# Grouped-query decode attention on one core: the V loads issued from GpSimd's queue, the K loads left on SyncE's

## The chip, the cores and the metric

The kernel runs on one core of a Trainium2 chip. The metric is the device time of one execution in microseconds (us); the text uses us throughout and MB for 10^6 bytes, MiB for 2^20. A profiled execution is read beside it: its span, engine by engine, and the DMA traffic. Engines are called TensorE (PE), VectorE (DVE), ScalarE (ACT), GpSimd (POOL) and SyncE (SP); 16 DMA engines move the data between the device's memory and the on-chip memory.

## The reference

Two sequences, one new token each. The token is normalised and goes through attention over a cache of 32768 keys and values, and through a small gated MLP; the results are multiplied and added to the token.

```python
# x (2,1,512); k_cache, v_cache (2, 8, 32768, 128) float32; 32 query heads, 8 K/V heads
xn = layernorm(x)
q  = (xn @ wq) split into 32 heads of 128
scores = q . k_cache * 128**-0.5          # 4 query heads share one K/V head
o  = softmax(scores) . v_cache
s  = o (all heads side by side) @ wo      # (4096, 512)
gate = xn @ W_gate ; gate = gate * (gate > 0)
g  = silu((gate * (xn @ W_up)) @ W_down)  # width 1792
out = x + s * g
```

Everything is float32. K and V together are 537 MB, read once; the weights are another 27 MB.

## The kernel before, in words

**Groups, tiles and pairs.** There are 16 groups, one for each sequence and K/V head. A group's 32768 tokens are 4 tiles of 8192. Tiles are handled two at a time: a *pair* j holds tiles 2j and 2j+1, so a group is two pairs and there are PAIRS = 32 of them. One load brings the K (or the V) of a whole pair, 8 MiB: 128 partitions with 64 KB each, in one contiguous piece per partition (`rows_of`, line 413).

**Buffers.** K has two buffers of 8 MiB, `kbuf[0]` and `kbuf[1]`, used in turn by even and odd pairs. V has one, `wide`. Before the first V, `wide` also serves the query weights `wq`, then the MLP's `W_gate` and `W_up`, then `W_down`. At the end the V of pair 30 goes into `kbuf[0]`, which has no more K to hold, and the output weights `wo` go into `kbuf[1]`, cut into six loads.

**A step.** The loop of line 882 takes one pair of scores and one pair of sums over V per step; sums run two pairs behind scores. In step j:

- VectorE transposes the K of pair j in place, 8 pieces (`k_transpose`, line 657), TensorE multiplies them with the query (`scores`, line 662);
- TensorE adds up the V of pair j-2 with the softmax weights (`values`, line 739);
- VectorE takes the scores out (`take_scores`); in every odd step a group is complete, and its maximum, its exponentials (ScalarE) and the sums and output of the group before follow (`tile_maximum`, `sums`, `maximum`, `take_o`, `finish_group`);
- the weights of the next sums are multiplied out on TensorE and transposed on VectorE (`weights`, `take_weights`).

**What GpSimd does.** In odd steps it forms the query of the next group (`take_query`, line 526, after the last scores of the old one) and copies a finished group's output into `ots` (line 810). Besides some preparation at the start it has nothing else.

**What sets the order.** Each operation is recorded by `Program.op` with the keys that it reads and writes; from these the class derives the semaphore waits. Each engine executes its own operations in the order in which they were recorded, and an operation that has to wait holds up all that come behind it on the same engine. A load is an operation of the engine that issues it: that engine waits until the destination is free, then hands the load to its DMA queue. The loads are recorded through one helper, with SyncE as the engine unless another is given:

```python
def load(dst, src, sem, r=(), w=(), engine="SP"):
    pg.op(engine, lambda e: e.dma_start(dst, src), r, w, dma=sem)
```

In step j the loads are recorded at the end of the step: the V of pair j-1 (`load_vv(j - 1)`, into `wide`, free once `values` of pair j-2 is done), then the K of pair j+2 (`load_kk(j + 2)`, free once `scores` of pair j is done). In step 30 the V of pairs 29 and 30 are loaded, in step 31 the V of pair 31 and `wo`. Only the two small loads of x at the start are issued elsewhere, by ScalarE.

## Time and profile before

| | |
|---|---|
| runs, median of 3 (lowest to highest) | 1309.91 us (1309.86 to 1310.29) |
| span of the profiled execution | 1308.4 us |
| bytes read | 564.67 MB, 432 GB/s over the span |
| busy, share of the span | TensorE 859.0 us (66%), VectorE 718.1 us (55%), ScalarE 51.4 us (4%), GpSimd 10.5 us (1%) |
| K loads | 32, median 48.2 us from issue to landing |
| V loads into `wide` | 31, median 29.6 us from issue to landing |

The profiled execution has no time of its own besides its span; the median of the runs is 1.5 us above that span.

How to read the lines that follow. A line of the timeline has the start and the busy time in us, the engine, the line of the kernel, the operation, its output and input, and in brackets the idle time before it with what ended it. Line 240 is `load`, line 243 is `mm`, so every load and nearly every matmul carries one of these numbers, and one tells them apart by their tiles: `s<-k,qcur` are scores, `o<-w,wt` and `o<-k,wt` are sums over V, `m_ps` is a scratch bank. `SPq` and `ACTq` are the issues of loads on SyncE's and ScalarE's queues; their duration is that of the issue, not of the transfer. The lines by slice cut the span into 40 equal parts and give the busy share in tenths. A line of the windows gives a stretch, its length, the busy time of PE, its weight load, VectorE, ScalarE and GpSimd with their counts, then the granted clock, the DMA share and GB/s.

### The profile page before, as it was taken

What the parts mean: (1) busy time and instruction counts of PE and PEld (TensorE: products, weight loads), DVE (VectorE), ACT (ScalarE), POOL (GpSimd) and SP (SyncE); (2) the same over time, 40 slices, a digit from 0 to 9 for tenths busy, and PEclk for the clock granted to TensorE, in tenths of its full rate; (3) what the DMA queues carried; (4) which work ended last, traced back from release to release, by engine and by line L of the source; (5) the groups of instructions that cost most, each with busy time, mean ns of one, the idle gap of its engine ahead of it and who ended that gap; (6) DMA issues with size and microseconds to landing.
All of it is one profiled execution on the core that took longest, in us unless ns stands there. A gap on an engine that the chain in (4) does not pass through costs nothing.

```text
span 1308.4 us, 11146 instructions
## 1 busy us (share of the span) xinstructions
PE 859.0 (66%) x4720; PEld 211.5 (16%) x4720; DVE 718.1 (55%) x690; ACT 51.4 (4%) x133; POOL 10.5 (1%) x38
## 2 busy tenths in 40 slices
PE   3566675785666587576667667667665757865676
PEld 1111111211111121111111112121111112111121
DVE  3566654565655456664546666455665545656521
ACT  0001000000000000000000000000000000000000
POOL 0000000000000000000000000000000000000000
PEclk9677788878878887878898778798887889788788
DMA  9999999999999999999999999999999999999998
GB/s 417 423 438 435 437 431 441 425 439 429 437 429 439 435 433 441 429 441 427 439 429 437 429 439 435 433 441 429 441 427 439 429 437 429 439 435 433 439 431 357
DMA packets 10693, 564.79 MB, mean 432 GB/s; under 512 B 1195, under 2 KB 1211, under 8 KB 1597
## 3 DMA queue, kind: packets, MB, share of 16 engines
q1 hardware_dynamic: 10668, 564.67, 99.7%
q8 instruction: 6, 0.10, 0.0%
q14 instruction: 3, 0.02, 0.0%
q10 hardware_dynamic: 16, 0.01, 0.0%
HBM read 564.67 MB, written 0.00 MB: 432 GB/s over the span
## 4 chain that ended last, share of the span: by engine, by line
DMA 64%; DVE 17%; PE 15%; issue 4%; SPq 0%
DMA k<-in_A_k_cache_dram 58%; DVE k L660 17%; PE o L243 8%; PE s L243 6%; DMA k<-in_A_wo_dram 3%; DMA w<-in_A_wq_dram 2%; PE m_ps L243 1%; PE m_ps L693 0%; PE d L243 0%; SPq L240 0%; DVE gy L870 0%; DVE gy L872 0%
## 5 line engine op out<-in xcount | busy, mean ns | idle before, releaser
L243 PE MATMUL s<-k,qcur 128*32 128x512 f32 x2048 | 504.5, 710 | 370.5 <-DVE k L660 370.3
L660 DVE STREAM_TRANSPOSE k<-k 128x2048 f32<-128x2048 f32 x256 | 565.2, 2275 | 147.0 <-DMA k<-in_A_k_cache_dram 147.0
L243 PE MATMUL o<-w,wt 128*16 128x512 f32 x1984 | 245.5, 596 | 9.0 <-DMA w<-in_A_v_cache_dram 9.0
L243 PEld LDWEIGHTS s<-k,qcur 128*32 128x32 f32 x2048 | 89.5, 123 | 785.0 <-DVE k L660 639.3
L737 DVE STREAM_TRANSPOSE wt<-pt 128x512 f32<-128x512 f32 x64 | 45.9, 717 | 139.4 <-PE pt L243 134.6
L678 DVE TENSOR_SCALAR_CACHE_REDUCE st<-s 128x512 f32<-128x512 f32 x64 | 43.0, 672 | 120.9 <-PE s L243 120.9
L243 PEld LDWEIGHTS o<-w,wt 128*16 128x16 f32 x1984 | 62.4, 98 | 167.5 <-issue 167.5
L722 ACT ACTIVATE st<-st,nb 128x512 f32<-128x512 f32 x64 | 45.4, 710 | 1111.0 <-DVE nb L719 1111.0
L243 PE MATMUL pt<-st,perm 128*128 128x512 f32 x128 | 72.6, 696 | 1.5 <-ACT st L722 1.5
L763 DVE RECIPROCAL rl<-m_ps 128x1 f32<-128x1 f32 x16 | 2.7, 169 | 111.0 <-PE m_ps L243 111.0
L243 PE MATMUL m_ps<-ob,heads 128*128 128x128 f32 x128 | 21.7, 321 | 29.0 <-DVE ob L777 29.0
L243 PEld LDWEIGHTS pt<-st,perm 128*128 128x128 f32 x128 | 25.3, 219 | 34.4 <-issue 30.1
L803 DVE STREAM_TRANSPOSE os<-m_ps 128x512 f32<-128x512 f32 x16 | 11.5, 717 | 23.2 <-PE m_ps L243 23.2
L243 PEld LDWEIGHTS m_ps<-ob,heads 128*128 128x128 f32 x128 | 18.0, 217 | 31.1 <-DVE ob L777 31.1
L243 PE MATMUL m_ps<-w,wt 128*32 128x512 f32 (+1 forms) x128 | 16.2, 640 | 8.1 <-DMA w<-in_A_wq_dram 8.1
L777 DVE SCALAR_TENSOR_TENSOR ob<-o,share,ob 128x128 f32<-128x128 f32 x48 | 16.9, 351 | 1.7
L530 POOL TENSOR_TENSOR qcur<-qall,block_of 128x128 f32<-128x128 f32 x16 | 6.5, 406 | 1008.3 <-PE s L243 974.0
L243 PE MATMUL m_ps<-negone,mrow 1*128 1x1 f32 x32 | 6.0, 256 | 9.3 <-DVE mrow L708 9.3
L722 ACT ACTIVATION_READ_ACCUMULATOR st<-st,nb 128x1 f32 x64 | 11.9, 186 | 0.0
L481 DVE COPY os<-m_ps 128x512 f32<-128x512 f32 x2 | 1.4, 692 | 16.3 <-PE m_ps L243 16.3
L243 PE MATMUL o<-k,wt 128*16 128x512 f32 x64 | 8.4, 687 | 2.8 <-DMA k<-in_A_v_cache_dram 2.8
L391 PE MATMUL m_ps<-ident,st 32*128 32x32 f32 x4 | 0.7, 307 | 14.0 <-DVE st L380 14.0
(80 smaller groups left out, 102.8 us busy)
## 6 DMA issues: line engine op xcount, KB each, us to landing
k<-in_A_wo_dram SPq DMA_DIRECT2D x1, 4096.0 KB, 37.3
w<-in_B_W_gate_dram SPq DMA_DIRECT2D x1, 3584.0 KB, 19.6
w<-in_B_W_up_dram SPq DMA_DIRECT2D x1, 3584.0 KB, 27.6
w<-in_B_W_down_dram SPq DMA_DIRECT2D x1, 3584.0 KB, 15.6
k<-in_A_wo_dram SPq DMA_DIRECT2D x1, 2048.0 KB, 41.7
k<-in_A_wo_dram SPq DMA_DIRECT2D x1, 1024.0 KB, 43.7
k<-in_A_k_cache_dram SPq DMA_DIRECT2D x32, 48.2
k<-in_A_wo_dram SPq DMA_DIRECT2D x1, 512.0 KB, 44.5
```

The source lines that it names most:

```text
L243: return lambda e: e.matmul(out_, lhs, rhs, start=start, stop=stop, skip_group_check=True)
L391: lambda e, k=k: e.transpose(px[:, k * 32 : (k + 1) * 32], xquad[:, k, :], ident[:32, :32])
L481: dve(lambda e, q=qs, h=half: e.tensor_copy(q, pq[h]), [f"m{half}"], [f"os{half}"])
L530: lambda e: e.tensor_tensor(qcur.rearrange("p e (k h) -> p e k h", h=REP), qall[:, b, hk].unsqueeze(2).to_broadcast([P, 4, Q // REP, REP]) ...
L660: dve(lambda e: e.transpose(at_, at_), [f"k{t // 2 % 2}"], [key])
L678: lambda e: e.tensor_scalar(st[u], ps_s[t % 2], SCALE, None, op0=ALU.mult, op1=ALU.max, accum_out=mx[:, u : u + 1],),
L722: lambda e, u=u: e.activation(st[u], st[u], AF.Exp, bias=nb, scale=1.0, accum_out=ls[:, u : u + 1]),
L737: dve(lambda e: e.transpose(wt[t % 2], ps_p[t % 2]), [f"pt{t % 2}"], [f"wt{t % 2}"])
L763: dve(lambda e: e.reciprocal(rl, ps_m[1][:, :1]), ["m1"], ["rl"])
L777: lambda e, part=part, c=c: e.scalar_tensor_tensor(ob, part, share[:, c : c + 1], ob, op0=ALU.mult, op1=ALU.add),
L803: lambda e: e.transpose(ot, ps_m[1].rearrange("p (h q j) -> p j h q", h=REP, j=ROWS)),
```

## The change

The loads into `wide` that bring V are issued by GpSimd instead of SyncE. The loads of a step are gathered in `load_next` and recorded right behind the sums over V, ahead of the work that takes the scores out, instead of at the end of the step. Thereby a V load stands on GpSimd's queue behind the sums over V that it waits for and ahead of the copy into `ots`. The K loads, the V load of pair 30 (into `kbuf[0]`), the MLP's weights and `wo` stay on SyncE's queue, where no V load stands between them any more. Nothing else is changed: the same bytes go into the same buffers with the same waits.

```diff
         if 2 * j == NK - 4:
             load(kbuf[0], rows_of(vc, 2 * j), "k0", w=k_keys(0))
         else:
-            load(wide, rows_of(vc, 2 * j), "v", w=["wide"])
+            load(wide, rows_of(vc, 2 * j), "v", w=["wide"], engine="POOL")
...
+    def load_next(j):
+        if j == 0:
+            load_d()
+        elif j < PAIRS - 1:
+            load_vv(j - 1)
+        if j == PAIRS - 2:
+            load_vv(PAIRS - 2)
+        if j + 2 < PAIRS:
+            load_kk(j + 2)
+        if j == PAIRS - 1:
+            load_vv(PAIRS - 1)
+            load_wo()
+
...
         if summed:
             values(v)
             values(v + 1)
+        load_next(j)
         if live:
             take_scores(s)
             take_scores(s + 1)
...
             for t in (v + 2, v + 3):
                 weights(t)
                 take_weights(t)
-        if j == 0:
-            load_d()
-        elif j < PAIRS - 1:
-            load_vv(j - 1)
-        if j == PAIRS - 2:
-            load_vv(PAIRS - 2)
-        if j + 2 < PAIRS:
-            load_kk(j + 2)
-        if j == PAIRS - 1:
-            load_vv(PAIRS - 1)
-            load_wo()
```

## The prediction

> **What bounds the kernel now.** I read the page first, its slices and its chain, then the issues on SyncE's queue in order of time, then one pair of steps engine by engine, then the start.

> ```profile
> span 1308.4 us, 11146 instructions
> DMA  9999999999999999999999999999999999999998
> q1 hardware_dynamic: 10668, 564.67, 99.7%
> HBM read 564.67 MB, written 0.00 MB: 432 GB/s over the span
> DMA 64%; DVE 17%; PE 15%; issue 4%; SPq 0%
> w<-in_A_v_cache_dram SPq DMA_DIRECT2D x31, 29.6
> k<-in_A_k_cache_dram SPq DMA_DIRECT2D x32, 48.2
> w<-in_A_wq_dram SPq DMA_DIRECT2D x1, 21.9
> ```

> All 16 DMA engines are busy in every slice but the last, and one queue, SyncE's, carries practically every byte. Nothing computed sets the pace: the bytes do. So a change in who issues a load can hardly gain; it can lose, if it lets the engines run dry. The next rows are the issues of steps 24 to 26, of the first three V loads and of the last.

> ```profile
> 96.45 0.33 SPq L240 DMA_DIRECT2D w<-in_A_v_cache_dram  x1
> ...
> 137.72 0.33 SPq L240 DMA_DIRECT2D w<-in_A_v_cache_dram  x1
> ...
> 175.83 0.33 SPq L240 DMA_DIRECT2D w<-in_A_v_cache_dram  x1
> ...
> 985.77 0.33 SPq L240 DMA_DIRECT2D w<-in_A_v_cache_dram  x1
> 986.14 0.43 SPq L240 DMA_DIRECT2D k<-in_A_k_cache_dram  x1
> 1025.91 0.33 SPq L240 DMA_DIRECT2D w<-in_A_v_cache_dram  x1
> ...
> 1063.05 0.33 SPq L240 DMA_DIRECT2D w<-in_A_v_cache_dram  x1
> ...
> 1257.88 0.33 SPq L240 DMA_DIRECT2D w<-in_A_v_cache_dram  x1
> 1258.25 2.81 SPq L240 DMA_DIRECT2D k<-in_A_wo_dram  x6
> ```

> Two steps take 1063.05 - 985.77 = 77.28 us and bring four loads of 8 MiB, so a load alone costs the engines 19.32 us, 434 GB/s. Each engine gets 8 partitions of a load, 64 KB each; I call one a row, 19.32 / 8 = 2.415 us. The query weights, the first load and also 8 MiB, took 21.9 us to land: 2.6 us of start and landing lie beside the 19.3.

> In each step V goes out first and K right behind, on one queue, in order. V lands 29.6 us after its issue: it waits about 8 us for the rest of the K load before it, then runs alone. K lands at 48.2, 19 us behind V. Before V is the next K at about 9 us; that order, K, V, K, V, is what the change gives up. What each load has to meet:

> ```profile
> 996.14 17.66 DVE L660 STREAM_TRANSPOSE k<-k 128x2048 f32<-128x2048 f32 x8 [7.74 <-DMA k<-in_A_k_cache_dram]
> 1018.42 0.59 PE L243 MATMUL s<-k,qcur 128*32 128x512 f32 x1
> 1018.42 7.46 PE L243 MATMUL o<-w,wt 128*16 128x512 f32 x61
> 1031.15 1.58 DVE L737 STREAM_TRANSPOSE wt<-pt 128x512 f32<-128x512 f32 x2
> 1034.81 17.67 DVE L660 STREAM_TRANSPOSE k<-k 128x2048 f32<-128x2048 f32 x8 [2.08 <-DMA k<-in_A_k_cache_dram]
> 1055.14 0.61 PE L243 MATMUL o<-w,wt 128*16 128x512 f32 x3
> 1055.56 0.59 PE L243 MATMUL s<-k,qcur 128*32 128x512 f32 x1
> 1064.11 1.58 DVE L737 STREAM_TRANSPOSE wt<-pt 128x512 f32<-128x512 f32 x2 [7.22 <-PE pt L243]
> ```

> Step 25 (odd): transposes begin at 996.14, scores end at 1019.0 (22.9 us), the sums over V end at the next issue, 1025.9 (6.9), VectorE is through the softmax of the group at 1032.7 (6.8). Step 26 (even): 1034.81, scores end at 1056.15 (21.3), sums end at 1063.05 (6.9), VectorE is through at 1065.7 (2.6). Together 67.4 us; the other 9.8 of 77.2 are the two waits for K, 7.74 and 2.08. K therefore has slack. V has almost none: issued at 1025.91 it lands at about 1055.5, and its first matmul stands at 1055.14; the one issued at 985.77 lands at about 1015.4, some 3 us ahead of its use.

> **The change part by part.** *Waits of the loads.* K's buffer is free when the scores end, V's when the sums end. Before, both went out at the end of the sums, for K stood behind V on SyncE. Now K goes out 6.9 us earlier, V where it did. PE, VectorE and ScalarE keep their programs.

> The start shows an issue on a third engine and two queues at work:

> ```profile
> 0.74 0.39 SPq L240 DMA_DIRECT2D w<-in_A_wq_dram  x1
> 1.42 1.19 ACTq L240 DMA_DIRECT2D st<-in_A_x_dram  x1
> 10.13 0.68 DVE L364 TENSOR_REDUCE stat<-st 32x1 f32<-32x512 f32 x1 [2.91 <-DMA st<-in_A_x_dram]
> 22.77 9.20 PE L243 MATMUL m_ps<-w,wt 128*32 128x512 f32 x64 [8.10 <-DMA w<-in_A_wq_dram]
> ```

> *GpSimd's queue.* A V load waits there for the sums. Ahead of it in an odd step is the next query's product, which needs the scores only; behind it stands the copy into `ots`, which needs VectorE's work after the same sums. Nobody waits longer for either: 0. The issue itself has no row on GpSimd. The nearest are 0.33 us on SyncE and 1.19 on ScalarE; I take at most 0.9 us more than now and count it with the 2.6 above. Below 0 it can't be: GpSimd starts no earlier than the sums end. [...]

> *Two queues instead of one.* This is the large term. What a DMA engine does with work on two queues shows only in the rows above. The 4 KB of x, issued behind the weights on ScalarE's queue, are in use at 10.13, while the weights go on until 22.7. The engine does not finish a load before it turns to the other queue; it changes after a row or two. [...] With V and K both waiting I therefore give each every second row, and V half the rate as long as K has rows.

> The steady pair, t = 0 at the end of the sums of an even step. V goes out. K went out 6.9 us ago and has 5 of 8 rows left. Five of each take 24.1 us. The next scores end at 2.6 + 22.9 = 25.5, the next K goes out, and V's last rows (1.4 us alone, then some 2.5 rows alternating with K) end at about 36.5; with 2.6 it lands at 39.1. Sums until 46.0, VectorE until 52.8, scores at 74.1, sums at 81.0 if the V issued at 46.0 is there: K has 1.6 rows left by then, so 9.6 rows and 2.6 us, landed at 71.8. It is. Two steps: **81.0 instead of 77.28, +3.7**. If each turn goes K first and landing costs a row more, 83; if V's turns come first, 79.8. In this pair the engines are dry some 4 us: K has nothing to fetch, both its buffers being full.

> Steps 2 and 3 cost more, as K's rows never run out behind the MLP's weights. V0 goes out at 96.5; 15 rows and 2.6 are 38.8: landed at 135.3 to 138, sums end at 142 to 145 (before: 137.72). V1: the same again, sums end at 188 to 194 (before: 175.83): +12 to +18, I take 16.

> Steps 4 to 31 are 14 pairs: 14 x 3.7 = 52.

> The end: now the last sums of step 31 end at 1257.9, and 50.5 us remain to 1308.4.

> ```profile
> 1286.06 9.01 PE L243 MATMUL o<-w,wt 128*16 128x512 f32 x64 [8.97 <-DMA w<-in_A_v_cache_dram]
> ...
> 1304.21 0.64 PE L243 MATMUL s<-k,ots 128*32 128x128 f32 x16 [0.17 <-DMA k<-in_A_wo_dram]
> ...
> 1306.60 0.69 SPq L240 DMA_DIRECT2D out_dram<-gy  x1
> ```

> Then the output weights go out 6.9 us earlier and V31 is the last to land, 25.8 us after the sums; 9.0 of sums, and 12 to 13.4 from there (before: 1295.1 to 1308.4, the last weights at 1304.2): 47 to 48, so -3.

> Sum: 1308.4 + 16 + 52 - 3 = 1373.4 us of span. The runs' median is 1309.91, 1.5 above the span, so 1374.9. With 79.8 to 83 for a pair and 12 to 18 at the start it is 1354 to 1405. Each landing that comes later than reckoned lengthens the loop and none shortens the rest, so I go 3 us above: **1378**.

> **The rivals.** *V first.* If a packet from GpSimd's queue holds its engine's whole share (8 rows) against single rows of K, V passes everything. V then lands 22 us after issue; K pays: some 10 of the K before it (issued one bare step of 34 us ago, 19.3 of them V's and 5 its predecessor's), two V loads, itself 19.3 and 1.5 to land, 69 us from the end of scores to the transposes two steps later, and 21.3 more: 90.7. The next two steps make do with the bare chain, 67.4. Four steps are 158 instead of 154.6; seven such cycles and a late K at the start, +25 to +55: 1335 to 1365; with packets of 2 to 4 rows both have nearly what they need, 1313 to 1335. For it: V's slack is the smaller. Against: the weights and x changed after a row or two. [...]

> *V starved.* If V's packets are a fraction of a row, K takes nearly all until it is empty. V issued at 0 starts at 12.4, stops at 25.5 for the next K, and lands at 25.5 + 19.3 + 6.2 + 2.6 = 53.6 instead of 39.1: up to 95 us for two steps, +18 in 14 pairs, 1570; with half rows a good third of it, from 1420. Against: both loads have 64 KB in one piece.

> *No change: whole loads in turn.* If an engine takes a load as a whole, V comes behind the rest of K(j+1) and ahead of the K issued 6.9 us before it, exactly as now. It lands 29 to 31 us after issue, and 1307 to 1312 stands. It decides from where V lands within about 31 us. Against: x at 10.13. [...]

> ```profile
> 100.00:138.00 38.00, 28.17 (x150) 6.50 (x145) 22.19 (x21) 4.58 (x10) 0.41 (x1) 0.82 1.01 438
> DVE k L660 <- DMA k<-in_A_k_cache_dram: 147.0, 31, 7.7
> ```

> *Faster.* If two queues close the seams between loads, the rate (last column, GB/s) would have to rise from 434: all bytes at the 438 of this stretch are 12 us less. But the queue is never empty now, and VectorE's 147 us of waits for K are no loss while the engines are full. That the change doesn't do what it says I see no way to: K and V have separate semaphores and buffers.

> **How the numbers follow.** Equal rows 0.53 (1354 to 1405, and to 1425 with landings later than reckoned), V first 0.20, V starved 0.10, no change 0.13, of which 0.01 falls beyond 0.2% on the slow side, faster 0.04. 0.2%, 2.6 us, is about what a measurement of this kernel can tell from no change. Leaving out faster, the low third of no change and nearly all of V starved is 0.17: the range is 1308 to 1430, and equal rows' own is 1354 to 1425. Faster 0.04, same 0.12, slower 0.53 + 0.20 + 0.10 + 0.01 = 0.84.

> **What would show it.** V's time to landing: 37 to 40 us in one step and 24 to 27 in the next (equal rows), 22 throughout (V first, then K at 40 to 70), about 30 (no change). PE's first matmul over V should wait for the V load, some 13 us in every second step, and VectorE's waits for K should be nearly gone (equal rows); DMA's slices should show 8 among the 9s. I am wrong if the engines stay full and V lands within 31 us.

## The result, and the profile after

The changed kernel is slower: the ratio is 1.0994, 95% interval 1.0976 to 1.1012. The profiled execution took 1443.3 us with a span of 1441.7. The median of its four runs, 1454.67, is no measure of the change, as two of them ran at a lower granted clock (0.77 and 0.80 against 0.82), and the ratio leaves those out. By the ratio the change costs some 130 us, 1440 us in place of 1309.9; later sections compare with this 1440. Forecast were 1378 us with a range up to 1430: the right side and the expected mechanism, but only half of its size, 68 us instead of 130.

The page of the changed kernel, then its longest waits on a load (total us, how many, the longest):

```profile
span 1441.7 us, 11146 instructions
DMA  9999998989899897998989899798989989899893
q1 hardware_dynamic: 6204, 304.62, 49.5%
q0 software_dynamic: 4464, 260.05, 42.1%
w<-in_A_v_cache_dram POOLq DMA_DIRECT2D x31, 35.5
k<-in_A_k_cache_dram SPq DMA_DIRECT2D x32, 33.9
...
PE o L243 <- DMA w<-in_A_v_cache_dram: 278.3, 17, 18.4
DVE k L660 <- DMA k<-in_A_k_cache_dram: 14.3, 2, 8.4
```

The bytes are the same, but the engines now have 7s and 8s among their slices. V is on a queue of its own (q0): 31 loads of 128 rows and 16 completions each are 4464 packets, so a V row is still one piece of 64 KB, like K's. The waits have changed sides: VectorE waited 147.0 us for K before, now 14.3; TensorE waits 278.3 us for V, before 9.0 and that at the end. V comes late in every second step, by 17.6 to 18.4 us in all but the first two and the last two of these steps. One pair of steps, GpSimd and TensorE and VectorE in order of time:

```profile
745.30 0.53 POOL L240 DMA_DIRECT2D w<-in_A_v_cache_dram  x1 [29.85 <-PE o L243]
765.24 3.62 PE L243 MATMUL s<-k,qcur 128*32 128x512 f32 x26 [1.15 <-DVE k L660]
768.95 0.40 POOL L530 TENSOR_TENSOR qcur<-qall,block_of 128x128 f32<-128x128 f32 x1 [23.12 <-PE s L243]
786.65 8.73 PE L243 MATMUL o<-w,wt 128*16 128x512 f32 x64 [17.79 <-DMA w<-in_A_v_cache_dram]
795.73 0.59 POOL L240 DMA_DIRECT2D w<-in_A_v_cache_dram  x1 [26.38 <-PE m_ps L243]
802.24 17.62 DVE L660 STREAM_TRANSPOSE k<-k 128x2048 f32<-128x2048 f32 x8
822.95 7.45 PE L243 MATMUL o<-w,wt 128*16 128x512 f32 x61
830.70 0.53 POOL L240 DMA_DIRECT2D w<-in_A_v_cache_dram  x1 [29.83 <-PE o L243]
```

This is the loop of the prediction. V goes out at 745.30 and TensorE begins with it at 786.65, 41.3 us later; the scores were done at 768.9, so it waits 17.8 us. Sums until 795.73, VectorE until 802.24, scores until 823.5, sums until 830.70. Two steps take 85.4 us instead of 77.28. The windows of that pair, and of a stretch just before it, in which K's buffers are both full (share of DMA and GB/s stand last):

```profile
745.30:830.70 85.40, 51.09 (x278) 11.82 (x277) 43.71 (x40) 2.93 (x8) 1.73 (x4) 0.82 0.92 393
...
720.00:738.00 18.00, 14.07 (x74) 2.64 (x76) 15.02 (x9) 0.00 (x0) 0.00 (x0) 0.85 0.69 295
```

The engines work 92% of the pair: the bytes no longer set the pace, the loop through V's one buffer does.

The trace also records the single packets of the DMA engines, and there the turns can be read one by one. From 749.3 on each engine moves a row of V, a row of K, a row of V and so on, 64 KB and 2.42 us each. V's eighth and last row is through by 783.9, a row of K follows, and only then, by 786.3, comes the 4-byte packet that ends V's load; TensorE begins at 786.65. On the way K's queue spends one of its turns, at 771.0 to 771.8, on the 4-byte packet of its own load. Counted from the row that was under way when V was issued, eight rows of K pass beside V's eight.

### The profile page after: what moved, and what is told of

Same layout as the page of the kernel before. It is cut to its first block, busy times and chain, and to the rows that moved or that the text cites. A ratio compares the mean times of both kernels' runs of the same rounds, so it can differ in the third digit from the quotient of the medians.

```text
span 1441.7 us, 11146 instructions
## 1 busy us (share of the span) xinstructions
PE 856.0 (59%) x4720; PEld 205.7 (14%) x4720; DVE 715.5 (50%) x690; ACT 51.4 (4%) x133; POOL 27.9 (2%) x69
## 3 DMA queue, kind: packets, MB, share of 16 engines
q0 software_dynamic: 4464, 260.05, 42.1%
HBM read 564.67 MB, written 0.00 MB: 392 GB/s over the span
## 4 chain that ended last, share of the span: by engine, by line
DMA 52%; issue 28%; PE 15%; DVE 6%; POOL 0%; SPq 0%; POOLq 0%; DVEq 0%
DMA w<-in_A_v_cache_dram 47%; PE o L243 11%; DMA k<-in_A_k_cache_dram 3%; DVE k L660 2%; PE m_ps L243 2%; DMA w<-in_A_wq_dram 2%; DVE ob L777 1%; PE s L243 1%; DVE os L803 1%; DVE ob L771 0%; DVE mrow L708 0%; DVE share L766 0%; PE pt L243 0%; PE m_ps L693 0%; DVE mr L698 0%
## 5 line engine op out<-in xcount | busy, mean ns | idle before, releaser
L243 PE MATMUL s<-k,qcur 128*32 128x512 f32 x2048 | 477.7, 646 | 239.7 <-DVE k L660 239.7
L660 DVE STREAM_TRANSPOSE k<-k 128x2048 f32<-128x2048 f32 x256 | 563.9, 2270 | 14.3 <-DMA k<-in_A_k_cache_dram 14.3
L243 PE MATMUL o<-w,wt 128*16 128x512 f32 x1984 | 260.4, 659 | 278.3 <-DMA w<-in_A_v_cache_dram 278.3
L243 PEld LDWEIGHTS s<-k,qcur 128*32 128x32 f32 x2048 | 84.6, 114 | 631.1 <-DVE k L660 511.4
L243 PEld LDWEIGHTS o<-w,wt 128*16 128x16 f32 x1984 | 60.8, 104 | 466.3 <-DMA w<-in_A_v_cache_dram 285.9
L737 DVE STREAM_TRANSPOSE wt<-pt 128x512 f32<-128x512 f32 x64 | 45.9, 717 | 147.5 <-PE pt L243 141.9
L243 PE MATMUL pt<-st,perm 128*128 128x512 f32 x128 | 68.7, 663 | 1.5 <-ACT st L722 1.5
L243 PE MATMUL m_ps<-ob,heads 128*128 128x128 f32 x128 | 20.4, 307 | 29.2 <-DVE ob L777 29.2
L240 POOL DMA_DIRECT2D w<-in_A_v_cache_dram x31 | 17.5, 565 | 884.4 <-PE o L243 472.9
L243 PEld LDWEIGHTS pt<-st,perm 128*128 128x128 f32 x128 | 23.6, 205 | 32.6 <-issue 27.2
L243 PEld LDWEIGHTS m_ps<-ob,heads 128*128 128x128 f32 x128 | 17.1, 208 | 31.4 <-DVE ob L777 31.4
L243 PE MATMUL m_ps<-w,wt 128*32 128x512 f32 (+1 forms) x128 | 15.4, 612 | 7.9 <-DMA w<-in_A_wq_dram 7.9
L243 PE MATMUL m_ps<-negone,mrow 1*128 1x1 f32 x32 | 6.0, 256 | 10.2 <-DVE mrow L708 10.2
```

Source lines behind the costliest of these rows:

```text
L243: return lambda e: e.matmul(out_, lhs, rhs, start=start, stop=stop, skip_group_check=True)
L660: dve(lambda e: e.transpose(at_, at_), [f"k{t // 2 % 2}"], [key])
L737: dve(lambda e: e.transpose(wt[t % 2], ps_p[t % 2]), [f"pt{t % 2}"], [f"wt{t % 2}"])
```

## The experiments

The theory: with V and K on two queues each engine takes a row of the one, then a row of the other; V, which had no slack, gets half the rate as long as K has rows. Rival 1: GpSimd's way of issuing a load is what is slow. Rival 2: K goes out 6.9 us earlier, ahead of V, and that costs, whatever the queue.

**act_queue.** V by ScalarE instead of GpSimd (ScalarE's loop written out, so that it can hold the loads).

```diff
-            load(wide, rows_of(vc, 2 * j), "v", w=["wide"], engine="POOL")
+            load(wide, rows_of(vc, 2 * j), "v", w=["wide"], engine="ACT")
...
-            pg.emit("ACT", e, sems, loop=(NU, NK))
+            pg.emit("ACT", e, sems)
```

> The V loads are issued by ScalarE instead of GpSimd, at the same place in the order; everything else as in the changed kernel. Theory (two queues take turns row by row, so V runs at half rate while K has rows, and the loop V, sums, softmax, scores, sums grows from 77.3 to 85.3 us per two steps): it makes no difference which second engine issues; 1425 to 1450 us, V landing about 41 us after its issue in every even step. Rival 1 (GpSimd's way of issuing a load is what is slow): back to about 1310. Rival 2 (K issued ahead of V is what costs, whatever the queue): as slow as the changed kernel too.

Measured: 1438.65 us, ratio 1.0963 (1.0941 to 1.0985). V goes out at 747.70 and TensorE begins with it at 789.30: 41.6 us, as from GpSimd. Who issued on the second queue, GpSimd or ScalarE, made no difference here.

```profile
747.70 50.78 ACTq L240 DMA_DIRECT2D w<-in_A_v_cache_dram  x2
...
789.30 8.78 PE L243 MATMUL o<-w,wt 128*16 128x512 f32 x64 [17.75 <-DMA w<-in_A_v_cache_dram]
```

**all_gpsimd.** The other half of that question: one queue, but GpSimd's.

```diff
-        load(kbuf[b], rows_of(kc, 2 * j), f"k{b}", w=k_keys(b))
+        load(kbuf[b], rows_of(kc, 2 * j), f"k{b}" if j < 2 else f"kp{b}", w=k_keys(b), engine="SP" if j < 2 else "POOL")
...
-            load(kbuf[0], rows_of(vc, 2 * j), "k0", w=k_keys(0))
+            load(kbuf[0], rows_of(vc, 2 * j), "kp0", w=k_keys(0), engine="POOL")
```

W_down and wo got `engine="POOL"` in the same way.

> All loads from W_down on (K, V and the output weights) issued by GpSimd, V first and K right behind it as in the kernel before: one queue again, but GpSimd's. Theory (taking turns between two queues is what costs): no second queue, 1308 to 1316 us. Rival 1 (GpSimd's way of issuing costs): well above 1330. Rival 2 (early K): K is not early here, about 1310.

Measured: 1311.87 us, ratio 1.0013 (1.0003 to 1.0022). On the page of this kernel the engines are as full as before, and V and K land after 28.8 and 47.6 us, the same order as on SyncE (29.6 and 48.2):

```profile
DMA  9999999999999999999999999999999999999998
q0 software_dynamic: 9808, 532.16, 93.8%
w<-in_A_v_cache_dram POOLq DMA_DIRECT2D x31, 28.8
k<-in_A_k_cache_dram POOLq DMA_DIRECT2D x30, 47.6
```

Rival 1 falls: GpSimd issues 94% of the bytes and loses 0.1%.

**moved_only.** Only the recording of the loads is moved; V stays on SyncE.

```diff
-            load(wide, rows_of(vc, 2 * j), "v", w=["wide"], engine="POOL")
+            load(wide, rows_of(vc, 2 * j), "v", w=["wide"])
```

> Only the second half of the change: the loads are recorded behind the sums over V, but V stays on SyncE. Every theory: the loads keep their order on SyncE and their waits, so 1308 to 1312 us, as before.

Measured: 1310.04 us, ratio 1.0001 (0.9991 to 1.0010). That half of the change does nothing by itself.

**k_held.** Two queues, but K leaves at the same moment as V, as before the change.

```diff
-        load(kbuf[b], rows_of(kc, 2 * j), f"k{b}", w=k_keys(b))
+        load(kbuf[b], rows_of(kc, 2 * j), f"k{b}", w=k_keys(b), after=["o"])
```

`after` makes the load wait for what last wrote the key, here the sums, and holds up nobody itself; V of pair 30 and wo got it too.

> V on GpSimd's queue as in the changed kernel, but each K load, the V load of pair 30 and the output weights also wait for the sums over V of their step, so that K and V go out at the same moment, as in the kernel before. Theory: V (8 rows) and the K just issued (8 rows) alternate from the first row in every step, V needs 38.6 + 2.6 = 41 us each time, then 9 us of sums: about 50 us a step instead of 42.7, 1570 to 1650 us. Rival 2 (it is the early K that costs): back to about 1310. Rival 1 (GpSimd's issue): about 1440, unchanged.

Measured: 1693.91 us, ratio 1.2915 (1.2893 to 1.2938); forecast were 1570 to 1650.

```profile
718.35 0.59 POOL L240 DMA_DIRECT2D w<-in_A_v_cache_dram  x1 [27.10 <-PE m_ps L243]
...
759.19 9.91 PE L243 MATMUL o<-w,wt 128*16 128x512 f32 x64 [10.43 <-DMA w<-in_A_v_cache_dram]
...
769.44 0.53 POOL L240 DMA_DIRECT2D w<-in_A_v_cache_dram  x1 [45.04 <-PE o L243]
```

V needs 759.19 - 718.35 = 40.8 us, now in every step (8 + 8 rows are 38.6, and 2.6), and a step takes 51.1. Rival 2 falls as the main cause: the early K is the better of the two ways to run two queues. The forecast was short in two ways. Its own 50 us a step in place of 42.7 come to some 1660 us over 30 steps, more than its range allowed; and the step took 1.1 us more than 50, most of it in the sums, 9.9 us here and not 9.

**one_queue_k_first.** K as early as in the changed kernel, on one queue.

```diff
-            load(wide, rows_of(vc, 2 * j), "v", w=["wide"], engine="POOL")
+            load(wide, rows_of(vc, 2 * j), "v", w=["wide"])
...
-        elif j < PAIRS - 1:
-            load_vv(j - 1)
         if j == PAIRS - 2:
             load_vv(PAIRS - 2)
         if j + 2 < PAIRS:
             load_kk(j + 2)
+        if 0 < j < PAIRS - 1:
+            load_vv(j - 1)
```

> All loads on SyncE's queue, but in each step K stands ahead of V: K goes out when the scores end, V behind it when the sums end. So K is as early as in the changed kernel, with one queue. Theory: without a second queue nothing is shared; V stands behind the whole K in the same order of bytes, the queue stays full for the most part and only the end is longer, as V of the last pair now comes behind the output weights: 1320 to 1345. Rival 2 (K ahead of V costs): 1430 or more. Rival 1 (GpSimd's issue): about 1310 to 1330.

Measured: 1353.33 us, ratio 1.0307 (1.0266 to 1.0347), some 8 us beyond what was expected. TensorE waits for V here too:

```profile
PE o L243 <- DMA w<-in_A_v_cache_dram: 174.2, 26, 15.1
```

So rival 2 holds in part: K ahead of V costs 3.1% without any second queue, though not the 1430 us that it would need to explain the change; V then stands behind the whole K of its step. These 3.1% are no share of the 9.9%: on two queues V does not stand behind K but takes turns with it, and there holding K back made the time longer still.

**k_rows_32k, k_rows_16k, v_rows_32k.** The share itself. A load is cut into loads of half or a quarter of the columns, so that its rows have 32 or 16 KB; the bytes stay, and whoever uses a load waits for all its parts. The diff is that of K in halves; quarters, and V in halves, are made alike.

```diff
-        load(kbuf[b], rows_of(kc, 2 * j), f"k{b}", w=k_keys(b))
+        cut = 2 * HALF // 2
+        for i in range(2):
+            at_ = slice(i * cut, (i + 1) * cut)
+            w = k_keys(b) if i == 0 else [f"k{b}+{i}"]
+            load(kbuf[b][:, at_], rows_of(kc, 2 * j)[:, at_], f"k{b}", w=w)
```

> The changed kernel with each K load cut into two loads of half the columns, so that a K row is 32 KB while a V row stays 64 KB; same bytes, same buffers, the transposes wait for both halves. Theory: taking turns row by row now gives V two thirds of the rate instead of half; V needs 8 of its own rows and 8 half rows of K, 29 us, and lands after about 31.6 us instead of 41.3: 1325 to 1345 us. Rival 1 (GpSimd's issue) and rival 2 (early K): about 1440, unchanged, or slightly more for the additional loads.

> The changed kernel with each K load cut into four loads of a quarter of the columns: K rows of 16 KB against V rows of 64 KB. Theory (turns row by row): V gets four fifths of the rate, 10 row times for its 8 rows, and lands after some 27 us; V is then no longer late in most steps, K is slower but has slack: 1325 to 1350 us, less than the 1361 of the halves. If only the number of loads mattered, it would be above 1361.

> The changed kernel with each V load cut into two loads of half the columns (rows of 32 KB) and K whole (64 KB); the sums wait for both. Theory (turns row by row): V gets a third of the rate while K has rows; V issued in an even step lands after about 49 us instead of 41, and the one of the odd step is late too: 85 us a pair become 93 or more, 1530 to 1620 us. If the engines shared by bytes, or if smaller pieces were simply better (as the K halves and quarters might suggest), it would be 1440 or less.

Measured: K's rows at 32 KB 1361.36 us, ratio 1.0392 (1.0362 to 1.0422); at 16 KB 1331.0, 1.0158 (1.0141 to 1.0175); V's at 32 KB 1540.11, 1.1732 (1.1683 to 1.1780). One pair of issue and use from K at 32 KB, and then one from V at 32 KB (an issue there is two loads):

```profile
749.68 0.59 POOL L240 DMA_DIRECT2D w<-in_A_v_cache_dram  x1 [17.77 <-PE m_ps L243]
783.30 9.54 PE L243 MATMUL o<-w,wt 128*16 128x512 f32 x64 [5.83 <-DMA w<-in_A_v_cache_dram]
```

```profile
703.84 1.05 POOL L240 DMA_DIRECT2D w<-in_A_v_cache_dram  x2 [30.48 <-PE o L243]
...
752.55 8.34 PE L243 MATMUL o<-w,wt 128*16 128x512 f32 x64 [25.12 <-DMA w<-in_A_v_cache_dram]
```

From issue to use V takes 33.6 us against half rows of K (31.6 to landing was forecast; the median landing of that run is 32.7), 41.3 against whole ones, and 48.7 when its own rows are halved (49 forecast). Smaller pieces are not better by themselves: halving K's gains 80 us, halving V's loses 100. In these runs the engines took turns by rows, not by bytes, and the load with the smaller rows gave way. The times of the quarters and of V's halves lie in their ranges; the halves of K, 1361 us, were expected at 1345 at most. V was still waited for in 25 of 31 steps there, 168.7 us in all. With K at 16 KB the waits have gone over to K again, in part:

```profile
w<-in_A_v_cache_dram POOLq DMA_DIRECT2D x31, 28.4
DVE k L664 <- DMA k<-in_A_k_cache_dram: 105.3, 14, 15.3
PE o L243 <- DMA w<-in_A_v_cache_dram: 69.5, 17, 16.4
```

It is the best of the kernels with two queues, and still 21 us behind the kernel before, with V and then K on one queue.

**kv_halves.** Both cut at 32 KB, and each half of V (one tile) goes out and is waited for by itself. K's loads are cut as above.

```diff
-        return half_of(wide, t), "wide"
+        return half_of(wide, t), f"wide_v{t % 2}"
...
-            load(wide, rows_of(vc, 2 * j), "v", w=["wide"], engine="POOL")
+            for i in range(2):
+                at_ = slice(i * HALF, (i + 1) * HALF)
+                w = ["wide_v0", "wide"] if i == 0 and j == 0 else [f"wide_v{i}"]
+                load(wide[:, at_], rows_of(vc, 2 * j)[:, at_], f"v{i}", w=w, engine="POOL")
```

> The changed kernel with K and V both cut into two loads of half the columns, one tile each: rows of 32 KB on both queues, K's transposes wait for both halves, but each half of V goes out when the sums of its own tile are done and is waited for by those sums alone. Theory: turns are equal as in the changed kernel, but V's loop gets shorter by the sums of one tile at both ends, 3.5 to 4.5 us each, about 8 us a pair: 85.3 back to 77.3, where the bytes set the pace again: 1315 to 1345 us. If it were the taking of turns as such (lost rate on the engines) and not V's loop, it would stay near 1440.

Measured: 1380.32 us, ratio 1.0535 (1.0517 to 1.0552), some half of the gain that was expected.

```profile
716.75 0.53 POOL L240 DMA_DIRECT2D w<-in_A_v_cache_dram  x1 [26.39 <-PE o L243]
720.18 0.53 POOL L240 DMA_DIRECT2D w<-in_A_v_cache_dram  x1 [2.90 <-PE o L243]
...
759.94 6.14 PE L243 MATMUL o<-w,wt 128*16 128x512 f32 x32 [12.73 <-DMA w<-in_A_v_cache_dram]
766.42 0.53 POOL L240 DMA_DIRECT2D w<-in_A_v_cache_dram  x1 [18.33 <-PE m_ps L243]
```

The first half leaves 3.4 us ahead of the second, as thought, and the rest of the sums takes 6.5 us instead of 9.1. So the loop is V's, and shortening it pays although the turns are equal. But half the matmuls take 70% of the time: 6.14 us for 32, where 64 take 8.7. TensorE is slow after the wait. That accounts for part of the missing gain; the rest stays open.

**pe_kept_busy, pe_busy_18.** Is it the idling? Matmuls of constants fill the wait, 144 and then 18 in each odd step.

```diff
+        if live and ends and j > 2:
+            spin = mm(ps_d[:32, :], fold, heads.rearrange("p h k m -> p (h k m)"), True, True)
+            pe(chain([spin] * 18), ["fold", "heads"], ["d"])
         if summed:
             values(v)
```

> The changed kernel with 144 matmuls of constants added on TensorE between the scores and the sums over V of each odd step, into a bank that nobody reads any more: they lie in the some 18 us in which TensorE waits for V. Theory for the sums' 8.8 us instead of 7.1: TensorE starts slowly after the idle time. Then the sums behind the added work take about 7.1, and 1.7 to 2 us go from each pair of steps: 25 to 32 us off the time. Rival (the sums are slow for another reason, such as reading V while K is written): 8.8 us remain and the time too.

> As pe_kept_busy, with the number of added matmuls set by what one of them took there (122.9 us for 144, 0.85 each): 18 of them, 15.4 us, inside the wait of some 18 us. Theory (TensorE starts slowly after idling): the sums over V of odd steps take about 7.4 instead of 8.8 us, 1.4 us for each of 15 pairs: 15 to 25 us off the changed kernel's time. Rival (slow for another reason): no change.

Measured: 3029.6 us with 144, for one takes 0.85 us, and not 0.25 like one of the sums (a pair's sums are 32 matmuls, which the trace lists as 64); 1439.85 with 18, ratio 1.0988 (1.0970 to 1.1006), which is the changed kernel's. One step of the first (the sums follow the added work without a gap), then one of the second:

```profile
875.45 0.61 PE L243 MATMUL o<-w,wt 128*16 128x512 f32 x3
...
875.89 7.44 PE L243 MATMUL o<-w,wt 128*16 128x512 f32 x61
```

```profile
772.82 15.18 PE L243 MATMUL d<-heads,fold 128*32 128x512 f32 x35
...
791.35 8.50 PE L243 MATMUL o<-w,wt 128*16 128x512 f32 x64 [3.35 <-DMA w<-in_A_v_cache_dram]
```

With no gap the 64 take 7.9 us from the first start to the last end (875.45 to 883.33; their first three run among the work before), with one of 3.35 us they take 8.5, with 17.8 us 8.7. The traces of all runs decide between idling and the rival. In all but kv_halves, whose sums come in halves, sums that start by themselves after an idle time of up to 2.0 us take 7.06 us, 23 times of 23 (one_queue_k_first at 710.01, after 1.70 us); after more than 3.5 us they take 8.3 to 10.0, 148 times of 148 (the changed kernel at 1214.10, 8.35 after 18.40 us; k_held at 759.19, 9.91 after 10.43); in between both occur. Sums that follow the scores are short while other loads are being written: the row of 7.45 us at 822.95 of the changed kernel, 61 of the 64, runs beside a DMA share of 0.99. So the idling does it in these runs, and 3 us of it were mostly enough: in 11 of the 13 steps in which the 18 matmuls left some 3 us, the sums still took 8.5 to 8.8, and the expected 15 to 25 us did not come. A filling that ends just as V lands was not tried.

**v0_first.** In step 1 the first V is put ahead of the next query on GpSimd.

```diff
-        elif j < PAIRS - 1:
+        elif 1 < j < PAIRS - 1:
             load_vv(j - 1)
...
                 if t == 2:
                     mlp_down()
+                    load_vv(0)
```

> The changed kernel, but in step 1 the first V load is recorded ahead of the next query's product, so that on GpSimd it waits for the MLP's last product only and not for the scores of the step. Theory: V0 goes out at about 96 us instead of 101.2, lands 5 us earlier, and the loop behind it starts 5 us earlier: 4 to 8 us off the time, as far as that shows. Rival (GpSimd's order costs nothing, as the prediction had it): no difference.

Measured: 1439.61 us, ratio 1.0989 (1.0971 to 1.1008): no difference. In the profiled execution V0 left at 95.60 instead of 101.17 and V1 at 146.81 instead of 153.96, but V2 left at 200.12, no earlier than the 198.47 of the changed kernel. The expectation was wrong: the lead was gone by the third V load. Why is not shown.

## Why the prediction was wrong in size

*What bounds the kernel, and that it could only lose*: right. *Rows in turn*: right, read from the packets themselves and shown from both sides: V is in use after 33.6, 41.3 and 48.7 us as K's rows are half of V's, equal and twice V's. The rivals *V first*, on a packet of 8 rows, *no change*, on whole loads, and *V starved*, on parts of a row, fall with the same three numbers. A full queue brought the same rate from GpSimd, 431 GB/s over the span of all_gpsimd, as from SyncE, 432 before; the time with V and K on two queues rose by 9.9% all the same.

*The steady pair* is the step that failed: 81.0 us forecast, 85.4 measured. Its mechanism was right, and two of its terms were too small, V's landing and, above all, the sums that had to wait for V. By its own terms:

| | forecast | measured |
|---|---|---|
| V from issue to use, even step | 39.1 | 41.3 |
| sums that had to wait | 6.9 | 9.1 |
| VectorE until the next transposes | 6.8 | 6.5 |
| transposes and scores | 21.3 | 21.3 |
| sums that had not | 6.9 | 7.2 |

V: the forecast had 15.1 row times up to V's last row (36.5 us), and 2.6 us for the landing. It was 16 row times and 2.7 us. I let K's queue run empty for 1.4 us, as scores of an odd step had taken 22.9 us before; without waiting for K they take 21.3 in both, and the next K left 23.6 us behind V. And I overlooked that the small packet that ends V's load waits for its turn like a row, behind one more row of K (783.9 to 786.3 in the pair above). This error alone lies within the bound of the prediction, 83, which allowed for a row more.

The sums: 6.9 us is the time from the end of the scores to the next V load when nothing is waited for. Such sums begin 1.0 us before the scores end (822.52 against 823.53 in the pair above) and take 7.9 us. Those that wait have no such lead, take 8.7 us because TensorE starts slowly (7.06 without that), and GpSimd begins the next load 0.35 us after they end (SyncE had needed 0.03): 9.1. The prediction itself quoted a row for sums that wait, 9.01 us for the last V, and used it for the end and not for the loop. The 0.3 us of GpSimd also stand in the last line of the table; the prediction had set them aside as at most 0.9.

4.4 us, 14 times, are 62 of the 68 us between the sum, 1374.9, and the 1443.3 of this execution. The 83 allowed for V's row more and left the sums at 6.9; both errors had the same sign.

*The start* was 16, and is 198.47 - 175.83 = 22.6:

```profile
101.17 0.72 POOL L240 DMA_DIRECT2D w<-in_A_v_cache_dram  x1
153.96 0.54 POOL L240 DMA_DIRECT2D w<-in_A_v_cache_dram  x1 [52.07 <-PE o L243]
...
198.47 0.59 POOL L240 DMA_DIRECT2D w<-in_A_v_cache_dram  x1 [20.49 <-PE m_ps L243]
```

"Nobody waits longer" on GpSimd's queue was wrong for one load: V0 needs the MLP's product only, and it stood behind the next query, which needs the scores. It left 4.7 us late; v0_first shows that this made no difference to the time. *The end* was -3 and is 1441.7 - 1395.64 - 50.5 = -4.4. *Steps 4 to 31* were 52 and are 115.1 (1395.64 - 198.47 against 1257.88 - 175.83). With the measured terms the sum gives the measured span, as it must: 1308.4 + 22.6 + 115.1 - 4.4 = 1441.7.

## What to carry to other kernels

Here two loads on one queue came one after the other, V 29.6 and K 48.2 us after the issue, and on two queues they shared, row by row; the load with no slack then came late, in use 41.3 us after its issue, though the other had slack to give. Before moving a load to another queue, look not at who issues it but at what stands on the other queue while it is in flight, and at whose rows are smaller. And price each instruction of a new loop by a row of the state in which the loop will find it: here TensorE's sums over a pair cost 9.1 us behind a wait, and 7.2 behind the scores.

## What the runs showed of the hardware

TensorE after an idle stretch of 17.8 us, its weight loads in the changed kernel (in brackets the idle time before each group of four):

```profile
789.19 0.17 PEld L243 LDWEIGHTS o<-w,wt 128*16 128x16 f32 x4 [0.68 <-issue]
790.04 0.13 PEld L243 LDWEIGHTS o<-w,wt 128*16 128x16 f32 x4 [0.68 <-issue]
790.50 0.11 PEld L243 LDWEIGHTS o<-w,wt 128*16 128x16 f32 x4 [0.32 <-issue]
790.93 0.11 PEld L243 LDWEIGHTS o<-w,wt 128*16 128x16 f32 x4 [0.32 <-issue]
```

From 786.65 to 790.5 a group comes every 0.85 us, from there on every 0.43: half speed for nearly 4 us. The granted clock was 0.54 from 786.65 to 790.40 and 1.00 from 790.50 to 795.30. In the traces of all runs, kv_halves left aside, the sums over V were short after up to 2.0 us of idling (7.06 us, 23 times of 23) and long after more than 3.5 (8.3 to 10.0 us, 148 times of 148); why the clock is lower behind such idling is not shown. In the kernel before, the sums over the V in `wide` followed the scores without a gap but for the last, 9.01 us after a wait of 8.97; in the changed kernel's loop the slow start lies on the path in every second step.
